# Half the rows of one late weight load, issued as thirty small transfers in two rounds

## The chip, the cores and the metric

The kernel runs on one core of one Trainium2 chip. The metric is the device time of the whole kernel in microseconds (us). A core has engines that run beside each other, each working through its own queue in order: TensorE (PE in the profile; PEld is its weight loads), VectorE (DVE), ScalarE (ACT), GpSimd (POOL) and SyncE (SP). They wait for one another by semaphores. Transfers between the chip's main memory (DRAM) and the on-chip memory are issued from SP's and POOL's queues and carried out by 16 DMA engines.

## The reference

Linear attention (feature map elu + 1), followed by a mix of 64 Fourier modes along the sequence and by a channel product:

```python
# q, k, v: (8 batches, 8 heads, 576, 64), all float32
phi = lambda x: np.where(x > 0, x, np.exp(x) - 1.0) + 1.0
q_p, k_p = phi(q), phi(k)
kv = np.einsum('bhsd,bhse->bhde', k_p, v)
num = np.einsum('bhsd,bhde->bhse', q_p, kv)
den = np.einsum('bhsd,bhd->bhs', q_p, k_p.sum(2))[..., None] + 1e-06
x = (num / den)                       # brought to (8, 576, 512)
X = np.fft.rfft(x, axis=1)            # the first 64 modes are used
# w_r, w_i: (64 modes, 512, 512) float32
Yr = np.einsum('bmd,mde->bme', Xr, w_r) - np.einsum('bmd,mde->bme', Xi, w_i)
Yi = np.einsum('bmd,mde->bme', Xr, w_i) + np.einsum('bmd,mde->bme', Xi, w_r)
u = x + np.fft.irfft(Y, n=576, axis=1)
out = u + np.maximum(u @ w_ch, 0.0)   # w_ch: (512, 512)
```

The two weight tensors `w_r` and `w_i` are 64 MiB each in float32. They are read once, and nearly all that the kernel reads is this.

## The kernel before

**Stages.** First the attention of the eight batches is worked out and brought into the Fourier domain (lines up to about L372). Then a loop runs over pairs of modes: `mode_pair(p)` for p = 0 to 30 and `last_pair()` for pair 31. Pair p needs the tile `w{p}`: 128 partition rows, one of 16 x 512 bfloat16 (16 KB) each. The even rows hold the two modes of `w_r`, the odd rows those of `w_i`. In DRAM a row is 32 KB of float32; the transfer casts it.

**How a weight tile is loaded.** `w_load(p, half, ...)` (L113) issues one transfer from POOL's queue for 64 of the 128 rows (`half` 0 is `w_r`, 1 is `w_i`), 1 MB as written. Below these two halves are called r(p) and i(p). `pin` keeps instructions in the order in which the program names them, so POOL issues r(28), i(28), r(29), i(29), r(30), i(30) and then the parts of pair 31, in this order. The last tile comes in eight transfers (`w_load_last`, L122): the fourth quarter is cut into five pieces (`PIECES`), so that the last product can start on the first of them.

**When it is loaded.** `w_get` (L408) is called at the start of a pair. From pair 5 on two buffers take turns (`W_KEEP = 2`), so the transfer r(p) must wait until the product of pair p-2 has read the buffer: POOL stands at that wait, and issues both halves one after the other when it ends. So while pair p is waited for, the transfers of pair p+1 at the most are queued behind it.

**What a pair does.** `mode_pair` (L462) runs 16 matmuls from the tile (`product`, L432), copies the result out (`evacuate`: DVE L447 for even p, ACT L449 for odd p), and then runs two slots of other work on TensorE: the attention rows, the fold of the early modes, and for the last pairs `form_z` (L726), `form_y` (L736) and `fold_lead` (L745 to L752) of the late modes. `keep_warm(FILL[p])` (L419) ends a pair with up to 12 matmuls whose result nobody reads.

**Last pair and tail.** `last_pair()` runs its first half, then the last matmuls `y_last` (L513) piece by piece as the pieces land. Everything after that depends on it: `last` (L932 to L943), two rearranging transfers `YZ_all` (L947, one on SP and one on POOL), and the output sums (L760, L800), which are stored by SP.

**Semaphores of POOL's transfers.** The built program has eight semaphores, DMASW0 to DMASW7, for the transfers that POOL issues, and takes them in turn. Where a transfer takes a semaphore whose earlier transfer has not been waited for already, POOL waits for that earlier transfer to land before it issues. In the kernel before r(28) has DMASW1, i(28) DMASW2, r(29) DMASW3 and i(29) DMASW4.

Of the kernel before, what the change touches and what calls it, by code (L numbers as in the profile page):

```python
# [43 lines left out]
def kernel(  # L44
# [10 lines left out]
    nc = tc.nc  # L55
# [7 lines left out]
    NDW = 4 * NDC  # L63
# [42 lines left out]
    pin = tc.keep_in_program_order  # L106
# [2 lines left out]

    LAST = NM // 2 - 1  # L110

    def w_load(p: int, half: int, pool, tag: str, bufs: int):
        if half == 0:  # L113
            w_in[p] = pool.tile([128, NDW, D], BF16, tag=tag, bufs=bufs, name=f"w{p}")
        two = (moe_w_r, moe_w_i)[half][2 * p : 2 * p + 2]
        pin(
            nc.gpsimd.dma_start(  # L117
                out=w_in[p][half::2], in_=two.rearrange("g (r dc) e -> (g r) dc e", dc=NDW)
            )
        )  # L120

    def w_load_last(pool, tag: str, bufs: int):  # L122
        w_in[LAST] = pool.tile([128, NDW, D], BF16, tag=tag, bufs=bufs, name=f"w{LAST}")
# [22 lines left out]
    def w_next():  # L146
        p, half = pending.pop(0)
        pool, tag, bufs = (wpool, "w", W_KEEP) if p < n_keep else (wpre, "wp", W_PRE)
        w_load(p, half, pool, tag, bufs)
# [258 lines left out]
    def w_get(p: int):  # L408
        if p not in w_in and p == LAST:
            w_load_last(wpool, "w", W_KEEP)  # L410
        elif p not in w_in:
            for half in range(2):
                w_load(p, half, wpool, "w", W_KEEP)
        return w_in[p]
# [174 lines left out]
    def x_of(t: int):  # L589
        if t < B * NJJ:  # L590
            return x_main[t // NJJ][:, t % NJJ, :]
        i = t - B * NJJ
        return x_tail[i // 2][:, i % 2, :]
# [352 lines left out]
    for h, eng in enumerate((nc.sync, nc.gpsimd)):  # L946
        eng.dma_start(  # L947
            out=YZ_all[64 * h : 64 * h + 64 : NF // NL].rearrange("r b z d -> r b (z d)"),
            in_=last.rearrange("p z d -> p (z d)"),
# [15 lines left out]
    def sums_of(n: int, i: int):  # L965
# [8 lines left out]
            out=x_of(0), in0=accs[0][:, 0], scalar=0.0, in1=x_of(0), op0=ALU.max, op1=ALU.add  # L974
# [50 lines left out]
```

## Time and profile before

| | us |
|---|---|
| median of 2 runs (421.56 to 422.1) | 421.83 |
| span of the profiled execution | 419.4 |
| PE busy | 317.2 (76%) |
| DVE busy | 231.3 (55%) |
| ACT busy | 154.2 (37%) |
| POOL busy | 57.4 (14%) |

| transfers | number, KB each | median us from issue to landing |
|---|---|---|
| w from `w_r`, pairs 0 to 30 (POOL) | 31 x 1024 | 13.2 |
| w from `w_i`, pairs 0 to 30 (POOL) | 31 x 1024 | 17.5 |
| w of pair 31: two halves of `w_r`, one of `w_i` (POOL) | 3 x 512 | 11.5 |
| w of pair 31: pieces of `w_i` (POOL) | 3 x 128 and 2 x 64 | 13.7 and 11.5 |

The engines' busy times overlap, so they do not add up to the span; what counts is which work the end waits for. The time from issue to landing is mostly time spent behind the transfers queued earlier. The median of the runs is 2.4 us over the profiled span; part of the device time lies outside the first and last instruction.

### The profile page before, as it was taken

To read this page: it belongs to the slowest core of one execution; us is meant where nothing else is said; L and a number is where in the kernel's file an instruction comes from. 1 tells how busy PE (TensorE), PEld (TensorE's weight loads), DVE (VectorE), ACT (ScalarE), POOL (GpSimd) and SP (SyncE) were. 2 spreads that over 40 slices of the span, in tenths; PEclk is the share of its full clock that TensorE was granted. 3 is DMA by queue.
4 is the path that set the end of the run, shared out by engine and by line. 5 is a ranking of instruction groups with operands and counts; after the bars stand their busy time and mean duration, and the time that the engine had idled before them with its cause. 6 is when DMAs were issued, how large, how long until landed. Compare 5 with 4: busy or idle time off the path is not lost.

```text
span 419.4 us, 7466 instructions
## 1 busy us (share of the span) xinstructions
PE 317.2 (76%) x3143; PEld 164.4 (39%) x3143; DVE 231.3 (55%) x509; ACT 154.2 (37%) x253; POOL 57.4 (14%) x100
## 2 busy tenths in 40 slices
PE   0369998999617875676767686988798877998993
PEld 0257776877301332222222233433343332453421
DVE  4588899785314563463645353464456443522794
ACT  4677798854201011000000233334253432330783
POOL 4222224210011211111111111111111111130000
PEclk9999999579855658665655599899899997899998
DMA  8999999999999999999999999999999999998698
GB/s 217 211 212 216 210 222 203 228 206 223 217 223 208 218 220 209 220 217 212 220 214 213 223 213 214 223 210 216 220 209 219 217 214 219 216 209 166 235 391 328
DMA packets 17073, 93.17 MB, mean 222 GB/s; under 512 B 2112, under 2 KB 3024, under 8 KB 12880
## 3 DMA queue, kind: packets, MB, share of 16 engines
q0 software_dynamic: 12496, 81.48, 93.4%
q1 hardware_dynamic: 4544, 11.22, 7.2%
q8 instruction: 24, 0.39, 0.3%
q14 instruction: 9, 0.07, 0.0%
HBM read 163.93 MB, written 9.44 MB: 413 GB/s over the span
## 4 chain that ended last, share of the span: by engine, by line
DMA 64%; PE 23%; DVE 4%; POOL 3%; ACT 3%; issue 2%; DVEq 0%; ACTq 0%; POOLq 0%
DMA w<-in_moe_w_i_dram 53%; DMA pick_sb<-row_pick 8%; PE P L432 6%; DMA k<-in_k_dram 3%; PE acc L760 3%; PE kvp L257 3%; PE acc L800 2%; POOL w L117 2%; PE z L726 1%; DVE x L293 1%; ACT ke L208 1%; PE xf L355 1%; PE zl L419 1%; PE qTp L237 1%; PE num L163 1%
## 5 line engine op out<-in xcount | busy, mean ns | idle before, releaser
L432 PE MATMUL P<-w,xz 128*32 128x512 bf16 x496 | 42.6, 475 | 37.6 <-DMA w<-in_moe_w_i_dram 35.4
L419 PE MATMUL zl<-wch,id 128*128 128x512 f16 x185 | 58.2, 466 | 0.0
L449 ACT CAST ys<-P 128x512 f16<-128x512 f32 x15 | 8.8, 586 | 132.4 <-PE P L432 132.4
L117 POOL DMA_DIRECT2D w<-in_moe_w_r_dram x31 | 17.3, 559 | 246.4 <-PE P L432 211.8
L447 DVE CAST ys<-P 128x512 f16<-128x512 f32 x17 | 11.8, 692 | 51.0 <-PE P L432 51.0
L706 PE MATMUL eps<-wch,xTw 128*128 128x512 f16 x144 | 39.3, 399 | 0.0
L432 PEld LDWEIGHTS <-xz 128*32 128x32 bf16 x496 | 12.6, 108 | 63.3 <-DMA w<-in_moe_w_i_dram 40.3
L163 PEld LDWEIGHTS <-qT 64*128 64x128 f16 (+1 forms) x640 | 22.6, 122 | 29.6 <-issue 15.6
L689 ACT CAST x16w<-x_main 128x512 f16<-128x512 f32 x32 | 19.8, 618 | 37.8 <-DVE x_main L687 37.8
L687 DVE TENSOR_TENSOR x_main<-ya,x_main 128x512 f32<-128x512 f32 x32 | 22.0, 689 | 16.5 <-PE ya L683 16.3
L257 PE MATMUL kvp<-vpad,ke 32*128 32x130 f16 x576 | 24.3, 263 | 8.9 <-ACT qT L244 6.1
L442 DVE COPY xz<-xt_c 64x256 bf16<-64x256 bf16 x62 | 23.0, 371 | 10.9 <-PE P L432 10.0
L419 PEld LDWEIGHTS <-id 128*128 128x128 f16 x185 | 18.9, 112 | 25.6 <-issue 14.3
L714 ACT CAST E<-eps 128x512 f16<-128x512 f32 (+1 forms) x40 | 21.2, 540 | 17.7 <-PE eps L706 17.7
L257 PEld LDWEIGHTS <-ke 32*128 32x128 f16 x576 | 22.3, 116 | 10.6 <-issue 8.6
L163 PE MATMUL nw<-kv_sb,qT 64*128 64x65 f16 (+1 forms) x320 | 18.2, 231 | 9.8 <-DVE x_tail L650 4.7
L237 PE MATMUL qTp<-id,qe 128*128 128x128 f16 x144 | 15.1, 289 | 10.6 <-DVE qe L221 9.5
L293 DVE TENSOR_TENSOR x<-num,rd 128x512 f16<-128x512 f32 x32 | 22.1, 692 | 1.1
L650 DVE TENSOR_TENSOR x_main<-nw,rd 128x256 f32<-128x256 f32 x32 | 11.2, 416 | 18.8 <-PE nw L163 18.8
L455 PE MATMUL yt<-pick_sb,ys 128*128 128x32 f16 (+1 forms) x128 | 8.8, 185 | 16.7 <-DMA pick_sb<-row_pick 9.4
L698 DVE COPY xTw<-xTp 128x512 f16<-128x512 f16 x36 | 15.0, 416 | 10.3 <-PE xTp L696 10.3
L208 ACT ACTIVATE qe<-q 128x1152 f16<-128x1152 f16 (+1 forms) x16 | 17.9, 1157 | 7.2 <-DMA q<-in_q_dram 7.1
(118 smaller groups left out, 507.5 us busy)
## 6 DMA issues: line engine op xcount, KB each, us to landing
w<-in_moe_w_r_dram POOLq DMA_DIRECT2D x31, 1024.0 KB, 13.2
w<-in_moe_w_i_dram POOLq DMA_DIRECT2D x31, 1024.0 KB, 17.5
out_dram<-x_main SPq DMA_DIRECT2D x12, 512.0 KB, 3.6
k<-in_k_dram POOLq DMA_DIRECT2D x8, 576.0 KB, 12.9
v<-in_v_dram POOLq DMA_DIRECT2D x8, 576.0 KB, 14.3
q<-in_q_dram POOLq DMA_DIRECT2D x7, 576.0 KB, 12.6
out_dram<-x_main SPq DMA_DIRECT2D x8, 256.0 KB, 4.0
q<-in_q_dram SPq DMA_DIRECT2D x2, 576.0 KB, 4.5
```

The lines of the kernel that those rows point to most:

```text
L117: nc.gpsimd.dma_start(out=w_in[p][half::2], in_=two.rearrange("g (r dc) e -> (g r) dc e", dc=NDW))
L163: mm = nc.tensor.matmul(num[hpo][orow, c0 : c0 + 65], qT[rows, hpp, h2, cols], kv_sb[rows, hpp, h2, :])
L208: pin(nc.scalar.activation(out=ev[:, c], in_=heads(nm, b, c), func=AF.Exp))
L257: nc.tensor.matmul(kv_ps[:, h2, 0:130], phi["k", b][r0 : r0 + 32, j // NJ, j % NJ].rearrange("p o d -> p (o d)"), vp[r0 : r0 + 32, :, j, 0 ...
L293: nc.vector.tensor_tensor(out=dst.rearrange("p (o c d) -> p o c d", o=2, c=4), in0=nv[:, :, :, 0:64], in1=rden.unsqueeze(3).broadcast_to([ ...
L419: pin(nc.tensor.matmul(last_ps[0], id16, wch16[:, 0, :]))
L432: nc.tensor.matmul(P[c : c + n, :], x, w[:, dc, :], start=(dc < NDC), stop=(dc >= n_dc - NDC), tile_position=(0, c), skip_group_check=True,)
L442: pin(nc.vector.tensor_copy(out=xz[p % 2][HALVES[h], :, h, :], in_=src))
L687: pin(nc.vector.tensor_tensor(out=x, in0=acc, in1=x, op=ALU.add))
L689: pin(nc.scalar.copy(out=x16w[t], in_=x))
L706: nc.tensor.matmul(e_ps, xT[:, c, :], wch16[:, c, :], start=(c == 0), stop=(c == NDC - 1))
L714: pin(nc.scalar.copy(out=dst, in_=e_ps[:, cols]))
```

## The change

One transfer, r(29), is issued differently; which bytes go where is the same. Its rows 0 to 31 go as one transfer. The other 32 rows are taken in two groups of 16 rows. A group is cut into small transfers of two rows each (the second group has three rows in its first and its last), and each small transfer moves only a part of its rows: in the first round of a group the first part of each of `h` pieces of a row, in the second round the rest. The length of the first part differs between the small transfers: 1/8, 2/8, 3/8, 5/8, 6/8, 7/8 of a row with `h` = 2, and 1/4 and 3/4 with `h` = 4. Group 1 makes 2 x 8 transfers and group 2 makes 2 x 7, so r(29) is issued as 31 transfers instead of one. i(29) and all the others are issued as before, behind these.

```diff
+    CUT = (29, 0)
+    WIDTHS = ((2, 1), (2, 2), (2, 3), (2, 5), (2, 6), (2, 7), (4, 1), (4, 3))
+    GROUPS = (
+        [(2, h, at) for h, at in WIDTHS],
+        [(3, 2, 1)] + [(2, h, at) for h, at in WIDTHS[1:6]] + [(3, 4, 1)],
+    )
+
     def w_load(p: int, half: int, pool, tag: str, bufs: int):
         if half == 0:
             w_in[p] = pool.tile([128, NDW, D], BF16, tag=tag, bufs=bufs, name=f"w{p}")
         two = (moe_w_r, moe_w_i)[half][2 * p : 2 * p + 2]
-        pin(
-            nc.gpsimd.dma_start(
-                out=w_in[p][half::2], in_=two.rearrange("g (r dc) e -> (g r) dc e", dc=NDW)
-            )
-        )
+        rows_in = two.rearrange("g (r dc) e -> (g r) dc e", dc=NDW)
+        if (p, half) != CUT:
+            pin(nc.gpsimd.dma_start(out=w_in[p][half::2], in_=rows_in))
+            return
+        pin(nc.gpsimd.dma_start(out=w_in[p][half : 2 * 32 : 2], in_=rows_in[0:32]))
+        lo = 32
+        for widths in GROUPS:
+            for part in range(2):
+                r0 = lo
+                for n, h, at in widths:
+                    dst = w_in[p].rearrange("p (h d) e -> p h d e", h=h)
+                    src = rows_in.rearrange("p (h d) e -> p h d e", h=h)
+                    ds = (slice(0, at), slice(at, NDW // h))[part]
+                    pin(
+                        nc.gpsimd.dma_start(
+                            out=dst[half + 2 * r0 : 2 * (r0 + n) : 2, :, ds, :],
+                            in_=src[r0 : r0 + n, :, ds, :],
+                        )
+                    )
+                    r0 += n
+            lo = r0
```

Below, the small transfers are called s1 to s30 in the order of their issue: s1 to s8 and s9 to s16 are the two rounds of the first group, s17 to s23 and s24 to s30 those of the second. In the built program POOL's instructions around r(29) are, with the semaphores that they wait for:

| instruction | takes | waits for |
|---|---|---|
| rows 0 to 31 of r(29) | DMASW3 | product of pair 27 |
| s1 to s5 | DMASW4 to 7, 0 | nothing |
| s6 | DMASW1 | r(28) landed |
| s7 | DMASW2 | i(28) landed |
| s8 | DMASW3 | rows 0 to 31 of r(29) landed |
| s9 to s30, each | the next in turn | the small transfer eight places earlier landed |
| i(29) | DMASW2 | s23 landed |
| r(30), i(30) | DMASW3, 4 | s24, s25 landed; r(30) also the product of pair 28 |

The order of the instructions on TensorE, VectorE, ScalarE and SyncE is as before; the product of pair 29 waits for more semaphores.

## The prediction

> **What bounds the kernel now.** I read the page first, for the busy DMA engines and the chain that ended last.
>
> ```profile
> span 419.4 us, 7466 instructions
> DMA  8999999999999999999999999999999999998698
> DMA 64%; PE 23%; DVE 4%; POOL 3%; ACT 3%; issue 2%; DVEq 0%; ACTq 0%; POOLq 0%
> ```
>
> The 16 DMA engines are busy in every slice until the last weight has landed, and the chain is mostly waits for weights. So what counts is whether the stream of transfers stays fed. Next, the chain in order of time, around the change:
>
> ```profile
> 331.40 17.46 DMA w<-in_moe_w_i_dram
> 348.90 1.07 PE P L432 x16
> ...
> 369.52 1.01 PE P L432 x16
> 370.52 0.29 issue
> 370.81 2.16 POOL w L129 x4
> 372.98 13.65 DMA w<-in_moe_w_i_dram
> 386.67 0.36 PE y_last L513 x8
> ```
>
> The end hangs on the last piece of pair 31, and that piece on the queue of transfers before it. Then POOL's timeline (start, length, instruction, idle before and its releaser):
>
> ```profile
> 340.64 0.54 POOL L117 DMA_DIRECT2D w<-in_moe_w_r_dram  x1 [8.70 <-PE P L432]
> 341.18 0.54 POOL L117 DMA_DIRECT2D w<-in_moe_w_i_dram  x1
> 350.26 0.54 POOL L117 DMA_DIRECT2D w<-in_moe_w_r_dram  x1 [8.54 <-PE P L432]
> 350.80 0.54 POOL L117 DMA_DIRECT2D w<-in_moe_w_i_dram  x1
> 361.59 0.54 POOL L117 DMA_DIRECT2D w<-in_moe_w_r_dram  x1 [10.24 <-PE P L432]
> ...
> 372.44 2.17 POOL L129 DMA_DIRECT2D w<-in_moe_w_i_dram  x4
> 378.34 0.54 POOL L129 DMA_DIRECT2D w<-in_moe_w_i_dram  x1 [3.74 <-DMA w<-in_moe_w_i_dram]
> 390.49 0.57 POOL L947 DMA_DIRECT2D YZ_all<-last  x1 [11.60 <-ACT last L943]
> ```
>
> A transfer of 1 MB and one of 64 KB (the last of L129) both hold POOL for 0.54 us: issuing has a price per transfer, not per byte. The line at 350.26 is r(29). When it is issued, r(28) and i(28) are the only work queued ahead. The line at 378.34 stands for a wait for a semaphore's earlier transfer: i(30) landed at 378.05 by the trace's completion records, so POOL goes on 0.29 us after a landing.
>
> The completion records, 16 per transfer (one per engine), give the rest. r(28): seven engines at 350.4 to 350.9, nine at 352.4 to 353.7. i(28): 355.2 to 358.63. i(29): the last at 368.27. The last piece of pair 31: 387.88. In steady state an engine needs 4.85 us for its four rows of a half, so 1.21 us a row; nine engines run up to 3.3 us behind the other seven.
>
> **The change, step by step, on the profiled run's clock.**
>
> 1. Up to 350.26 nothing differs. Rows 0 to 31 of r(29) go out at 350.26, s1 to s5 follow at 0.54 us each until 353.5, s6 waits for r(28) (353.71) and goes at 354.0. Cover for this: the fast engines have i(28) to move until 355.2.
>
> 2. s7 waits for i(28), the slowest engine at 358.63, and goes at 358.9. s8 waits for rows 0 to 31 of r(29): two rows on each engine, behind i(28). The fast engines end them at 355.24 + 2.42 = 357.7, the slowest at 358.63 + 2.42 = 361.05. So s8 issues at 361.05 + 0.29 = 361.34. Queued behind the waiting POOL are s9 to s30, i(29), r(30), i(30). This is the added wait: at 357.7 the fast engines have only fractions of a row from s1 to s7 left, and run dry.
>
> 3. From there POOL issues s8 to s30, 23 transfers, each possibly held by the one eight places back. From a POOL issue with nothing queued ahead (the line at 390.49) to its first packet at 392.47 the trace has 1.98 us; the longest part, 7/8 of a row, takes 1.06 us, and the wake 0.29: 3.3 us. Eight issues take 8 x 0.544 = 4.35 us, which is longer, so the issue is the bound. No row shows a transfer of 2 or 3 rows. The nearest are 64 rows in L129's 64 KB pieces, 0.544 us; q, k and v with 256 runs take 0.72 us, which by the slope between (0.92 ns a run) makes 0.49 us for the 4 to 12 runs of a small one. I take 0.544 as the nearest and keep 0.40 to 0.72 for the range. So 23 x 0.544 = 12.51 us, and i(29) is issued at 361.34 + 12.51 = 373.85 instead of 350.80.
>
> 4. i(29): first packet at 373.85 + 1.98 = 375.83, four rows 4.85 us, and 0.37 us more on the engines that still hold the end of s30 (issued 0.54 us earlier, 0.91 us for 3/4 of a row). It lands at 381.05, against 368.27: 12.8 us late. The laggards' 3.3 us are already counted, since every engine has waited by then.
>
> 5. Behind i(29) the stream is as before: r(30) and i(30) are issued right after it, their buffer being free since 361.3, and keep the engines busy until about 390.7; pair 31 is issued after product 29, at about 382.5, well ahead. From i(29)'s landing to the last piece the run of before has 387.88 - 368.27 = 19.61 us. New: 400.7.
>
> 6. TensorE: product 29 began at 369.45, 1.18 us after i(29) landed, since earlier work was still running; then TensorE was busy until product 30, but for 0.27 us. Now it stands idle from about 369.5 to 381. In a cold stretch of this trace the products take 1.90 us in place of 1.05 (at 124.9, after 9.4 us idle), and between 350 and 360 the granted clock is 0.66. If half the clock lasts 3.4 us (the shortest stretch among the clock's records) the work behind product 29 loses 1.7 us, if 6.8 us (the one from 351.9) 3.4 us; the slack is 1.18 + 0.27 = 1.45 us. So product 30 and with it y_last come 0.25 to 1.95 us late, or 0 if the clock stays. I take 0.6. The TensorE work between product 30 and y_last filled the time but for 0.4 us, so little of this is won back.
>
> The tail behind y_last is unchanged. Sum: 12.8 + 0.6 = 13.4 us. Span 419.4 + 13.4 = 432.8; the median stands 2.4 us above the profiled span: 435.2 us, 3.2% slower.
>
> The Trainium skill, "DMA: Bandwidth & Descriptors", section "Anatomy of one DMA — SWDGE (gpsimd) path", puts a dispatch at about 50 ns and descriptor generation as "small, variable". By it the 23 issues would be an estimated 1.2 us instead of 12.5 and the sum some 2 us. The rows speak against that price here: 62 weight issues of 0.52 us or more. The same page's "Rules for kernel authors" says that transfers under 64 KB are mostly overhead, which speaks against the change; these small ones write 4 to 42 KB.
>
> **The rivals.**
>
> Piling up (slower still). Which engines take two rows I can't see: all weight transfers shown have at least 64. If the two rows of every small transfer go to the same two engines, each of those moves 8 + 7 = 15 rows, 18.1 us, then its four rows of i(29): 361.05 + 18.1 + 4.85 = 384.0, 2.9 us later than step 4; with the higher end of step 6 439.5 us. Against: 64 rows are spread over all 16 engines, four each. The same price comes from a small transfer that takes 5.5 us in place of 3.3 to come back: (5.8 - 4.35) x 23/8 = 4.2 us more, 439.4 us.
>
> Not slower (within 2%). One mechanism: POOL is done with a small transfer much sooner than with any of before. The threshold is 8.4 us, so 5.0 of the 13.4 must go: 5.0/23 = 0.22, an issue of 0.327 us or less. At 0.1 us the sum is 12.8 - 10.2 = 2.6 us and there is no cold clock: 424.4 us. For it speaks that a small transfer has a dozen runs at most; against it that runs hardly count in the rows (0.544 us at 64, 0.72 at 256).
>
> The wait is no wait (the change doesn't do what the list says): if s7 and s8 didn't stop POOL, i(29) would go out at 350.80 + 30 x 0.544 = 367.1 and land 4.85 + 1.98 later, at 374.0 and 5.7 us late: 427.5 us, 1.4%. Against it stands the same kind of wait at 378.34.
>
> Faster: the most that could be won is the laggards' lead. Seven engines near 0, four at 2.1, five at 3.25 us behind make a mean of 1.6, so evening them out ends 1.7 us sooner, 0.4%. Every engine gets one whole row in each group by the row counts, so nothing is evened out, and by 2% no way leads.
>
> **How the numbers follow.** Issue-bound as summed: 0.70 (431 to 437.5). Piling up or long round trips: 0.20 (437 to 440). Cheap issue, or no wait: 0.09 (423 to 430). Faster by over 2%: 0.01. The range 430.5 to 439.5 takes in an issue of 0.40 us without cold clock (435.2 - 3.3 - 0.6 = 431.3), 0.72 us partly (+4.0 = 439.2), and both prices of the pile. Two per cent is 430.3; less than that I would not tell from no change. Slower 0.90, same 0.09, faster 0.01.
>
> **What would show it.** In the profile after: 30 short POOL issues, with an idle of some 4 us before the seventh (released by i(28)) and of 2 us before the eighth, then 22 back to back to about 373.9; DMA busy share and GB/s low for some 12 us from about 358 to 375; TensorE idle before product 29 for about 11 us; product 29 at about 381. After that everything as before, 13 us later. Wrong if POOL passes the small ones at under 0.33 us, if s7 and s8 issue without idle, or if the stream's dip is filled, which would need more than two tiles' transfers queued.

## The result, and the profile after

The changed kernel takes 435.83 us (435.7 to 435.96, 2 runs) against 421.83: a ratio of 1.0338, 95% interval 1.0318 to 1.0357. The forecast was 435.2 us.

The page of the changed kernel, with the span, the busy share of the DMA engines and the rate in 40 slices:

```profile
span 433.8 us, 7501 instructions
DMA  8999999999999999999999999999999992699698
GB/s 218 212 212 214 212 214 212 225 218 218 211 215 218 216 218 218 218 218 217 218 216 218 216 215 215 215 216 215 216 213 219 216 210 45 99 215 194 210 387 326
```

The same line of the kernel before:

```profile
GB/s 217 211 212 216 210 222 203 228 206 223 217 223 208 218 220 209 220 217 212 220 214 213 223 213 214 223 210 216 220 209 219 217 214 219 216 209 166 235 391 328
```

The stream of weights, which had no such hole before, has one of two slices: 45 and 99 GB/s instead of some 215. A slice is 10.8 us, so the hole lies between 358 and 380 us, and it is worth (1 - 45/215 + 1 - 99/215) x 10.8 = 14.4 us. The span grew by 433.8 - 419.4 = 14.4: the hole is as long as the loss.

POOL's timeline (start, length, instruction, idle before and its releaser; L127 issues rows 0 to 31, L137 the small transfers, L125 all the others) says who made the hole:

```profile
350.44 0.52 POOL L127 DMA_DIRECT2D w<-in_moe_w_r_dram  x1 [8.57 <-PE P L455]
351.01 2.75 POOL L137 DMA_DIRECT2D w<-in_moe_w_r_dram  x5
354.18 0.54 POOL L137 DMA_DIRECT2D w<-in_moe_w_r_dram  x1 [0.42 <-DMA w<-in_moe_w_r_dram]
359.11 0.54 POOL L137 DMA_DIRECT2D w<-in_moe_w_r_dram  x1 [4.39 <-DMA w<-in_moe_w_i_dram]
361.47 12.37 POOL L137 DMA_DIRECT2D w<-in_moe_w_r_dram  x23 [1.81 <-DMA w<-in_moe_w_r_dram]
373.83 0.56 POOL L125 DMA_DIRECT2D w<-in_moe_w_i_dram  x1
```

s7 stands 4.39 us at i(28), s8 1.81 us at rows 0 to 31 of r(29), and then 23 small transfers go out back to back: 12.37/23 = 0.538 us each, with no wait between them. Only then does i(29) get its turn, 23 us later than before. The chain in order of time now runs through POOL, where it ran through transfers alone before:

```profile
350.44 10.75 DMA w<-in_moe_w_r_dram
361.19 0.28 issue
361.47 12.19 POOL w L137 x23
373.65 0.18 issue
373.83 8.10 DMA w<-in_moe_w_i_dram
381.93 0.09 issue
382.02 1.92 PE P L455 x15
...
386.30 14.40 DMA w<-in_moe_w_i_dram
```

And the list of issues of the changed kernel between 350 and 380 us (the last number is the median from issue to landing) shows two of the round trips of small transfers, which for s8 to s30 all lie between 1.95 and 3.60 us, under the 8 x 0.538 = 4.3 us after which their semaphore is asked for again:

```profile
w<-in_moe_w_r_dram POOLq DMA_DIRECT2D x6, 8.0 KB, 2.3
...
w<-in_moe_w_r_dram POOLq DMA_DIRECT2D x3, 28.0 KB, 3.6
```

### The profile page after: what moved, and what is told of

Same layout as the page of the kernel before. It is cut to its first block, busy times and chain, and to the rows that moved or that the text cites. A ratio compares the mean times of both kernels' runs of the same rounds, so it can differ in the third digit from the quotient of the medians.

```text
span 433.8 us, 7501 instructions
## 1 busy us (share of the span) xinstructions
PE 316.9 (73%) x3143; PEld 164.7 (38%) x3143; DVE 231.0 (53%) x509; ACT 154.1 (36%) x253; POOL 72.8 (17%) x130
## 2 busy tenths in 40 slices
DMA packets 18673, 93.17 MB, mean 215 GB/s; under 512 B 3588, under 2 KB 4546, under 8 KB 14512
## 4 chain that ended last, share of the span: by engine, by line
DMA 70%; PE 13%; POOL 6%; DVE 4%; issue 3%; ACT 2%; DVEq 0%; ACTq 0%; POOLq 0%
DMA w<-in_moe_w_i_dram 53%; DMA pick_sb<-row_pick 8%; DMA k<-in_k_dram 7%; PE P L455 6%; PE acc L783 3%; POOL w L137 3%; DMA w<-in_moe_w_r_dram 2%; PE acc L823 2%; POOL w L125 1%; DVE x L316 1%; PE kvp L280 1%; ACT ke L231 1%; POOL w L152 0%; PE qTp L260 0%; DVE qe L244 0%
## 5 line engine op out<-in xcount | busy, mean ns | idle before, releaser
L125 POOL DMA_DIRECT2D w<-in_moe_w_r_dram x30 | 16.6, 553 | 228.4 <-PE P L455 194.7
L280 PEld LDWEIGHTS <-ke 32*128 32x128 f16 x576 | 22.6, 118 | 10.6 <-issue 8.2
L186 PE MATMUL num<-kv_sb,qT 64*128 64x65 f16 (+1 forms) x320 | 16.5, 220 | 5.6 <-DVE x L316 3.7
## 6 DMA issues: line engine op xcount, KB each, us to landing
q<-in_q_dram POOLq DMA_DIRECT2D x7, 576.0 KB, 12.8
```

Of the source, the lines that this page charges most:

```text
L125: pin(nc.gpsimd.dma_start(out=w_in[p][half::2], in_=rows_in))
L186: mm = nc.tensor.matmul(num[hpo][orow, c0 : c0 + 65], qT[rows, hpp, h2, cols], kv_sb[rows, hpp, h2, :])
L280: nc.tensor.matmul(kv_ps[:, h2, 0:130], phi["k", b][r0 : r0 + 32, j // NJ, j % NJ].rearrange("p o d -> p (o d)"), vp[r0 : r0 + 32, :, j, 0 ...
```

## The experiments

The kernels differ from the changed kernel in how r(29) or i(29) is issued; two (e6, e10) run more keep-warm matmuls instead. The theory was: time = (the moment at which POOL is let go) + (issues until the stream is full-size again) x (price of an issue) + a constant.

### One round of whole rows (e1)

```diff
-        for widths in GROUPS:
...
+        r0 = 32
+        for n in (2,) * 8 + (3,) + (2,) * 5 + (3,):
+            pin(
+                nc.gpsimd.dma_start(
+                    out=w_in[p][half + 2 * r0 : 2 * (r0 + n) : 2], in_=rows_in[r0 : r0 + n]
+                )
+            )
+            r0 += n
...
```

> The 32 rows go in one round of whole rows: 15 small transfers instead of 30. Theory (the delay is POOL held until rows 0 to 31 have landed, then one issue of 0.538 us per small transfer): s8 still issues near 361.4; 8 issues until s15, so i(29) issues at 361.4 + 8 x 0.538 = 365.7 and lands 8.1 later at 373.8, 5.5 us after the kernel before; TensorE idles only some 4 us, so 0 to 0.5 on top. Time 427 to 428.5. Rival A (moving rows in parts on two engines is what costs): all parts are gone, 421.8 to 423.5. Rival B (one lost refill of the queue, however many transfers follow): 434 to 436.

Measured: 435.12 us, ratio 1.0322 (1.0305 to 1.0339). The theory's range is missed by 6.6 us; the time is what rival B gives. POOL's timeline of e1 shows that B is not the reason either:

```profile
361.43 2.47 POOL L131 DMA_DIRECT2D w<-in_moe_w_r_dram  x5 [1.89 <-DMA w<-in_moe_w_r_dram]
364.55 0.50 POOL L131 DMA_DIRECT2D w<-in_moe_w_r_dram  x1 [0.65 <-DMA w<-in_moe_w_r_dram]
365.78 0.50 POOL L131 DMA_DIRECT2D w<-in_moe_w_r_dram  x1 [0.73 <-DMA w<-in_moe_w_r_dram]
367.01 0.51 POOL L131 DMA_DIRECT2D w<-in_moe_w_r_dram  x1 [0.73 <-DMA w<-in_moe_w_r_dram]
368.24 0.57 POOL L125 DMA_DIRECT2D w<-in_moe_w_i_dram  x1 [0.73 <-DMA w<-in_moe_w_r_dram]
```

From s13 on the issues come 1.23 us apart, the time of one row on one engine: each waits for the small transfer eight places earlier. In the completion records (16 increments per transfer, one per engine) a small transfer of this stretch has 14 increments together and two late ones, and these two come every 1.23 us. The trace doesn't name the engine of a packet, but this is what the same two engines moving nearly all of it would give: of the 32 rows they take 15 each, 15 x 1.23 = 18.4 us. Free of rows 0 to 31 at 357.7, they end their four rows of i(29) at 357.7 + 18.4 + 4.9 = 381.0; i(29) landed on 14 engines by 376.4 and on the last two at 381.0 and 381.4. This is the prediction's rival of piling up, met in a kernel of mine and not in the change.

The Trainium skill, "DMA: Bandwidth & Descriptors", section "Why a DMA increments its semaphore by 16 and not by 1", states two ways for transfers issued from GpSimd. As a rule a transfer runs on as many engines as the largest number up to 16 that divides the size of the slowest dimension on both sides, and fewer than 16 engines are taken in turn from a cursor that moves on. On trn2 some direct copies are instead dealt out over 16 engines with a sixteenth of the rows, rounded up, to each; the page doesn't say which copies. The runs fit both: two whole rows in one piece (two rows of 8192 elements) behave as if they came back to the same two engines each time. The changed kernel's rows in two or four pieces don't: the first packets of s1 to s5, told apart by their sizes, run at the same time on different engines between 357.2 and 357.8.

### Thirty transfers of whole rows (e2)

```diff
+        for n in (1,) * 28 + (2, 2):
...
```

> 30 small transfers as in the changed kernel, but of whole rows (28 of one row, 2 of two), no second round and no parts of different length. Theory (number of issues alone): i(29) issues at 373.8 as in the changed kernel, 435.2 to 436.4. Rival A (parts and rounds cost): 428 or less. Rival C (a transfer of few rows piles on few engines): a time that moves by over 2 us either way, since these are spread otherwise.

Measured: 434.83 us, ratio 1.0312 (1.0297 to 1.0328), 1.0 us under the changed kernel and 0.4 under the range given. POOL's timeline:

```profile
361.40 11.23 POOL L131 DMA_DIRECT2D w<-in_moe_w_r_dram  x23 [1.84 <-DMA w<-in_moe_w_r_dram]
372.59 0.60 POOL L125 DMA_DIRECT2D w<-in_moe_w_i_dram  x1
```

s8 to s30 take 11.23 us, 0.488 each, and i(29) goes out at 372.59, 1.24 us earlier than in the changed kernel. Its one-row transfers run as 1 KB packets on many engines at once. Two rounds, parts and their lengths don't make the loss; the number of issues does, with its price.

### Equal parts (e4)

```diff
-    WIDTHS = ((2, 1), (2, 2), (2, 3), (2, 5), (2, 6), (2, 7), (4, 1), (4, 3))
+    WIDTHS = ((2, 4),) * 8
-        [(3, 2, 1)] + [(2, h, at) for h, at in WIDTHS[1:6]] + [(3, 4, 1)],
+        [(3, 2, 4)] + [(2, h, at) for h, at in WIDTHS[1:6]] + [(3, 2, 4)],
```

> As the changed kernel with the same 30 transfers in two rounds, but every row cut into equal halves (h = 2, at = 4) instead of parts of different length. Theory: the lengths don't matter as long as a transfer is back within eight issues (4.3 us): 435.2 to 436.4. Rival A (uneven parts leave engines waiting for the longest): 430 to 434.

Measured: 436.64 us, ratio 1.0354 (1.0339 to 1.037), 0.2 above the range.

```profile
361.46 12.78 POOL L137 DMA_DIRECT2D w<-in_moe_w_r_dram  x23 [1.98 <-DMA w<-in_moe_w_r_dram]
374.25 0.57 POOL L125 DMA_DIRECT2D w<-in_moe_w_i_dram  x1
```

The issues take 12.78 us (0.556 each), i(29) goes out at 374.25. Equal parts win nothing, so the uneven lengths are not what costs.

### Seven transfers, piled and spread (e3, e9)

```diff
+        for n in (5, 5, 5, 5, 4, 4, 4):
...
```

e3 (above) moves whole rows; e9 (below) moves 16 rows with each transfer, a part of each row in two pieces (`h` = 2):

```diff
+        for r0, n, ds in [(32, 16, slice(d, d + 2)) for d in (0, 2, 4, 6)] + [(48, 16, slice(a, b)) for a, b in ((0, 2), (2, 5), (5, 8))]:
...
```

> The 32 rows in 7 transfers of 4 or 5 whole rows. Theory: i(29) has to wait for rows 0 to 31 (361.05) and issues at 361.3 to 361.5, before the slowest engines have done with r(29) at 363.4, so these never run dry: 421.5 to 422.8, no measurable difference from before, although the seven issues, the waits of s6 and s7 and the idle POOL are all there. Rival D (each small transfer costs its issue on the path): 7 x 0.54 = 3.8, so 425.6. Rival B (the wait for a landing is what loses the queue): 425 or more.

> The 32 rows in 7 transfers of 16 rows, each a part of the rows in two pieces, so that they are spread over 16 engines. Theory: i(29) issues at 361.4, when the slowest engines still have work until 363.4: 421.5 to 422.8, against 426.6 of e3, which had the same number of transfers, the same waits and the same moment of issue but whole rows, piled on the first four or five engines. Rival D (every small transfer costs its issue on the path) and rival B (the wait for a landing loses the queue): 425 or more, as e3.

Measured: e3 426.55 us, ratio 1.0122 (1.0107 to 1.0137); e9 423.22, ratio 1.0046 (1.0032 to 1.006). i(29) is issued at the same moment in both; from the POOL timelines of e3 and of e9:

```profile
361.38 0.57 POOL L125 DMA_DIRECT2D w<-in_moe_w_i_dram  x1 [1.74 <-DMA w<-in_moe_w_r_dram]
```

```profile
361.39 0.56 POOL L125 DMA_DIRECT2D w<-in_moe_w_i_dram  x1 [1.88 <-DMA w<-in_moe_w_r_dram]
```

So the 3.3 us between them are not POOL's. In e3 i(29) lands on twelve engines by 369.4 and on four at 371.2, 371.4, 371.5 and 373.1, as if four engines had taken a row of every one of the seven transfers; in e9 it lands on all by 369.23. The expectation for e3 was wrong for the reason found in e1. That for e9 was 0.4 us too low: seven issues, two waits and an i(29) that goes out 10.6 us later cost 1.7 us and not 3.8, but not nothing. The slowest engines do not stand still for long, but the first packet of i(29) takes 1.4 to 2.2 us on 15 of the 16 engines instead of 1.23, and it lands at 369.23 instead of 368.27; the other 0.6 us come later, on the way to the last piece (389.45 instead of 387.88).

### Sixteen transfers, spread (e8)

```diff
+        for r0, n, ds in [(r0, 4, ds) for g in (32, 48) for ds in (slice(0, 4), slice(4, 8)) for r0 in range(g, g + 16, 4)]:
...
```

> The 32 rows in 16 transfers: four rows each, in two rounds of half rows, each half taken as two pieces (h = 2, d 0 to 4 and 4 to 8), the form of the changed kernel, which there was spread over the engines. Theory (with the piling of e1 allowed for: whole rows in one piece go to the first engines, rows in two pieces are spread): s8 issues near 361.45, s8 to s16 take 9 x 0.54 = 4.9, i(29) issues at 366.3 and lands 8.1 later at 374.4, 6.1 us later than before: 427.5 to 429.5. If the number of issues doesn't matter and e1 was right as measured: 434 to 436.

Measured: 428.72 us, ratio 1.0168 (1.0153 to 1.0183), as the theory has it. POOL's timeline:

```profile
361.51 5.31 POOL L132 DMA_DIRECT2D w<-in_moe_w_r_dram  x9 [1.84 <-DMA w<-in_moe_w_r_dram]
366.82 0.57 POOL L125 DMA_DIRECT2D w<-in_moe_w_i_dram  x1
```

The two windows from 362 to 368 us, first of e1 and then of e8 (busy times of the engines, the clock, the DMA engines' busy share, GB/s), show the difference between 15 piled transfers and 16 spread ones:

```profile
362.00:368.00 6.00, 6.00 (x42) 2.49 (x35) 3.55 (x6) 2.77 (x5) 3.41 (x7) 1.00 0.16 30
```

```profile
362.00:368.00 6.00, 6.00 (x35) 3.03 (x35) 2.89 (x6) 2.73 (x5) 6.00 (x12) 1.00 0.42 47
```

A busy share of 0.16 is between two and three engines of 16, while POOL (the fifth engine, 3.41 of 6 us) waits; in e8 POOL is busy for all 6 us and is the bound.

### i(29) ahead of the small transfers (e5)

```diff
+        if (p, half) == (CUT[0], 1):
+            return
...
         pin(nc.gpsimd.dma_start(out=w_in[p][half : 2 * 32 : 2], in_=rows_in[0:32]))
+        other = moe_w_i[2 * p : 2 * p + 2].rearrange("g (r dc) e -> (g r) dc e", dc=NDW)
+        pin(nc.gpsimd.dma_start(out=w_in[p][1::2], in_=other))
...
```

> i(29) is issued right behind rows 0 to 31 of r(29), ahead of the 30 small transfers, so that 4.85 us more of full-size work lie queued in front of them. Theory (POOL may have eight transfers out, so s8 now waits for i(29) instead of rows 0 to 31): i(29) lands at 365.9 on the slowest engine, s8 issues at 366.2, s8 to s30 take 12.4, r(30) issues at 378.6 and i(30) lands at about 391.9 against 392.1 in the changed kernel: 435 to 436.5, nothing won. Rival E (a deeper queue hides the issues): 430.7, the 4.85 us less; with no wait for landings at all 425 to 427.

Measured: 436.84 us, ratio 1.0353 (1.0338 to 1.0369), 0.3 above the theory's range. The POOL timeline of e5:

```profile
358.98 0.55 POOL L141 DMA_DIRECT2D w<-in_moe_w_r_dram  x1 [3.98 <-DMA w<-in_moe_w_i_dram]
361.38 0.56 POOL L141 DMA_DIRECT2D w<-in_moe_w_r_dram  x1 [1.85 <-DMA w<-in_moe_w_r_dram]
366.26 12.79 POOL L141 DMA_DIRECT2D w<-in_moe_w_r_dram  x23 [4.33 <-DMA w<-in_moe_w_i_dram]
379.04 0.56 POOL L127 DMA_DIRECT2D w<-in_moe_w_r_dram  x1
```

4.85 us more of full-size work are queued in front, and POOL is held 4.8 us longer, since one of its eight semaphores now belongs to that work. The same 23 issues follow. A deeper queue ahead doesn't hide them: the wait moves along with it.

### A warm TensorE (e6, e10)

```diff
-    FILL = {**{p: 7 for p in range(5, 16)}, **{p: 7 for p in range(18, 27)}, 27: 7, 28: 10, 29: 12, 30: 10}
+    FILL = {**{p: 7 for p in range(5, 16)}, **{p: 7 for p in range(18, 27)}, 27: 7, 28: 70, 29: 12, 30: 10}
```

e10 has 28: 60.

> The changed kernel with 60 more keep-warm matmuls after pair 28, which fill TensorE's idle of 13.9 us before product 29. Theory (step 6: the cold clock costs what is left of it after the slack, measured 0.3 us as product 30 starting 0.31 after i(30) has landed): product 29 takes 1.05 in place of 1.90 us, product 30 starts within 0.1 us of the landing, time 0.2 to 0.5 us under the changed kernel in the same call. Rival F (the cold clock costs its whole loss): 1.5 to 2.5 us under it. Rival G (it is hidden): no difference beyond 0.2.

> The changed kernel with 50 more keep-warm matmuls after pair 28 instead of the 60 of e6, which ran on past the landing of i(29) and so delayed product 29 themselves. At 0.218 us each they end near 379, before i(29) lands at 381.9, so product 29 should take 1.05 us. If the cold clock costs the changed kernel at most the 0.3 us by which product 30 was late in one of its two profiles, 435.4 to 436.1; if it costs 1.5 us or more, 434.3 or less. If the code loaded for the added matmuls holds one engine back as in e6, where the last increment of i(29) came 1.2 us behind the others, up to 437.

Measured: e6 437.62 us (435.82 to 438.87), ratio 1.0368 (1.0333 to 1.0403), inconclusive: the added matmuls ran past i(29)'s landing (product 29 at 383.88), a code packet ran on one engine at 379.2, and the last increment of i(29) came at 383.04, the others by 381.9, and the clock was half from 402.6 to 406.0, in the tail. e10: 436.26 us, ratio 1.0352 (1.0335 to 1.0369), 0.2 above its first case. Its TensorE timeline, products 29 and 30:

```profile
381.69 1.05 PE L455 MATMUL P<-w,xz 128*32 128x512 bf16 x16 [1.31 <-issue]
...
391.39 1.05 PE L455 MATMUL P<-w,xz 128*32 128x512 bf16 x16 [1.31 <-DMA w<-in_moe_w_i_dram]
```

The changed kernel itself was run once more with e5 and e6 (435.82 us, ratio 1.0328, 1.031 to 1.0345):

> The changed kernel once more, for comparison on the same chip: 435.2 to 436.4, i(29) issued near 373.8, and product 30 about 0.3 us after i(30) has landed.

```profile
381.89 1.90 PE L455 MATMUL P<-w,xz 128*32 128x512 bf16 x16 [13.79 <-DMA w<-in_moe_w_i_dram]
...
392.16 1.05 PE L455 MATMUL P<-w,xz 128*32 128x512 bf16 x16 [0.29 <-DMA w<-in_moe_w_i_dram]
```

Product 29 is cold in it, 1.90 us after 13.8 us of idle, and product 30 nevertheless waits 0.29 us for its weights. The granted clock is 0.50 from 372.9 to 386.6 us in the changed kernel's first profile, and 1.00 in all of this stretch in e10's. The warm clock gives a longer wait there (1.31) and no time. In e10's profile the last piece did land 0.8 us sooner, 401.25 against 402.05, but not by the clock: i(29) landed 0.3 us sooner (381.60 against 381.93), and no code packet (last section) falls between it and 400.7, where the changed kernel has one that makes one engine 0.5 us late. The last output store landed at 432.58 against 432.61, so nothing of this was left; why e10's tail took 0.8 us longer isn't shown.

### All spread runs together

| run | small transfers | us an issue | i(29) issued | time, us | time less the issue of i(29) |
|---|---|---|---|---|---|
| e9 | 7 | 0.50 | 361.39 | 423.22 | 61.8 |
| e8 | 16 | 0.59 | 366.82 | 428.72 | 61.9 |
| e2 | 30, whole rows | 0.49 | 372.59 | 434.83 | 62.2 |
| changed kernel | 30 | 0.54 | 373.83 | 435.83 | 62.0 |
| e4 | 30, equal parts | 0.56 | 374.25 | 436.64 | 62.4 |
| e3 (piled) | 7 | 0.52 | 361.38 | 426.55 | 65.2 |
| e1 (piled) | 15 | 0.50 | 368.24 | 435.12 | 66.9 |

In the five spread runs the time follows the moment at which i(29) is issued to within 0.6 us, over 13 us. The kernel before took 421.5 to 421.8 us beside each of them. Where the rows pile up, 3 to 5 us come on top.

## Why the prediction was right, step by step

- Steps 1 and 2 (POOL is let go when rows 0 to 31 have landed): s8 was forecast at 361.34 and issued at 361.47, the idle before s7 and s8 at 4 and 2 us and measured at 4.39 and 1.81. e5 shows that it is the eight semaphores: another transfer in front moves the wait by that transfer's time. More than eight semaphores, or a third buffer for the weight tiles, weren't tried.
- Step 3 (issues back to back, price per transfer): 12.51 us forecast, 12.37 measured. The row taken as the nearest, 0.544 us for 64 rows, came close to the 0.538 measured, and that is partly luck: the same 23 issues took 0.488 each with whole rows (e2), which is the 0.49 of the extrapolation, and 0.556 with equal parts (e4). The number of pieces doesn't set the price, since e8 with eight pieces a transfer took 0.59 and e9 with 32 pieces 0.50; what sets it between 0.49 and 0.59 no run shows. e9, e8 and the changed kernel, with 7, 16 and 30 transfers, give 1.01 us of time for each us by which the issue of i(29) is moved: (435.83 - 423.22) / (373.83 - 361.39).
- Step 4 (i(29) lands at 381.05) was 0.9 us short: 381.93. Its first packet came sooner than taken, 1.26 us after the issue instead of 1.98, but the first packet on most engines took 2.0 to 2.4 us instead of 1.23, and four engines, three of which had the end of s30, started i(29) only between 376.2 and 376.6. From issue to landing it was 8.10 us, not 7.20.
- Step 5 (19.61 us from there to the last piece): 402.05 - 381.93 = 20.12, 0.5 more. This is one engine: the last piece landed on the other 15 by 401.55, 19.62 us after i(29), and i(30) on 15 by 391.70 and on the last at 392.14. By the times of the packets that engine was held by a code packet (last section), for which the prediction had no term.
- Step 6 (cold clock, 0.6 us) is the term that failed: its cost is nothing that the runs show. The loss was sized well. First the products 29 and 30 of the kernel before, then those of the changed kernel with the second group of `y_last`:

```profile
369.45 1.05 PE L432 MATMUL P<-w,xz 128*32 128x512 bf16 x16
...
378.10 1.05 PE L432 MATMUL P<-w,xz 128*32 128x512 bf16 x16 [0.27 <-DMA w<-in_moe_w_i_dram]
```

```profile
382.02 1.90 PE L455 MATMUL P<-w,xz 128*32 128x512 bf16 x16 [13.86 <-DMA w<-in_moe_w_i_dram]
...
392.45 1.05 PE L455 MATMUL P<-w,xz 128*32 128x512 bf16 x16
...
400.75 0.36 PE L536 MATMUL y_last<-xl,w 128*128 128x16 bf16 x8 [0.24 <-DMA w<-in_moe_w_i_dram]
```

  From the start of product 29 TensorE works 8.38 us until it is free for product 30 before and 10.43 us after, 2.05 us more in this profile, between the 1.7 and 3.4 us of the step. But a late product 30 is not on the path: it came 0.31 us after its weights in one profile and waited 0.29 us for them in the other, with the same time, and `y_last` waited for its piece in both (0.24 us above). e10 without the cold clock is not faster.
- The sum: 12.8 + 0.6 = 13.4 us forecast; 13.7 to i(29)'s landing (381.93 - 368.27), 0.5 to the last piece and 0.2 in the tail measured, 14.4 in the span. The hit is partly luck: steps 4 and 5 were 1.4 us short together and step 6 was 0.6 too long. It is 1.0 us off in the span and 0.6 in the median, which stands 2.1 us above the profiled span instead of 2.4.
- The rivals. "Not slower" by cheap issues fell with 0.538 us; the Trainium skill's price in "DMA: Bandwidth & Descriptors", section "Anatomy of one DMA — SWDGE (gpsimd) path", of about 50 ns for a dispatch is not what an issue holds POOL for here. "The wait is no wait" fell with the idle before s7 and s8. Piling up is real (e1, e3), but takes whole rows in one piece; the changed kernel's pieces are spread. "Faster" by evening the engines out: the spread did fall, from 3.3 us (364.9 to 368.3) at i(29) to 0.9 (381.05 to 381.93), since all engines had run dry; the price was the hole. (The mean lead in that rival, 1.6 us, is 1.5 by its own terms; nothing rests on it.)

## What to carry to other kernels

Price a split of a transfer by the number of issues times what one issue holds the issuing engine (0.49 to 0.59 us here, whether it moves 4 KB or 1 MB), and ask how many transfers may be out at once: with eight semaphores, small transfers take the places that full-size ones need to keep the stream fed. Seven small transfers, which with rows 0 to 31 filled the eight places, cost little here (1.7 us); beyond them each issue cost its full time. Then look at which engines the pieces land on: a transfer of a few whole rows can go to the same few engines each time.

## What the runs showed that was not expected

- The form of the access pattern decides the engines. By the completion times, two or three whole rows in one piece went to the same two or three of 16 engines in all 15 transfers of e1 (two increments in 16 late, 1.23 us apart from transfer to transfer), and four or five rows in one piece to the same four or five in e3. Single whole rows were spread (e2), and so were four or 16 rows cut into two pieces (e8, e9).
- After the stream had run dry, the first 16 KB packets took 2.0 to 2.4 us instead of 1.23 on 12 of the 16 engines.
- A small transfer brings some 49 packets of under 512 B with it: (3588 - 2112) / 30 by the profiles of the two kernels. They are 4 bytes each in the trace's list and take 7 to 22 ns, and no run shows a cost of them apart from the issue.
- One code packet (16 KB of the queue that the profile calls instruction, 0.95 us) holds one DMA engine. In both profiles of the changed kernel one starts at 388.25 or 388.27, in a stretch where all engines run level. By the times of the packets around it, one engine ends a weight packet then and starts its next at 389.2, 0.92 us late, and this next one takes 1.41 us instead of 1.23; the last increments of i(30) and of the last piece are 0.4 and 0.5 us behind the other 15 (step 5). In e6 such a packet at 379.2 puts the last increments of i(29), r(30) and i(30) some 1.2 us behind the other 15. In the kernel before one at 375.22 leaves the same gap of 0.92 us. That these packets are also what makes nine engines late there (24 of them, 22.7 us in all) would fit the sum of their lags, 4 x 2.1 + 5 x 3.25 = 24.7 us, but no run tests it.
